# The last head pair's rows, stored in transfers of 64 rows and loaded with sixteen rows outermost

## The chip, the cores and the metric

The kernel runs on one core of a Trainium2 chip. The metric is the device time of one execution in microseconds (us). The kernel before was run three times: 1737.94 us at the median, from 1737.83 to 1739.5. A separate execution was recorded by the hardware profiler; all numbers of the trace are from it.

The engines in the tables are PE (TensorE, matrix multiplications; PEld is its loading of weights), DVE (VectorE), ACT (ScalarE), POOL (GpSimd) and SP (SyncE, which here only issues transfers). The data of every transfer is moved by sixteen DMA engines that the core has, whichever engine issues it.

## The reference

The output mixes two branches of the same input `x` (2048 x 512) by a gate per row:

```
g = sigmoid((x * gate_w).sum(-1))
q, k, v = heads(x @ wqkv)                    # 32 heads of 16
a = softmax(q k^T / 4) v, heads joined, @ wo # (2048 x 512)
b = Re(DFT over rows and columns of x)       # by matrices, (2048 x 512)
out = g * a + (1 - g) * b
```

The change touches only the last step of the branch `a`: the way in which the attention's result `o` of the last heads reaches the multiplication with `wo`.

## The kernel before

**Precision.** A float32 operand is split into a high part and a low part (names with `h` and `l`), and a product is made of three: high by high, high by low, low by high. So each operand of the output projection comes as a pair of blocks, each of 128 partitions by 512 columns.

**Attention.** The 32 heads are worked on in 16 pairs `p`, each in two halves `h` of 1024 queries, each half in 16 blocks of keys. One step is one such block: PE makes the scores (line 210), ACT their exponentials (lines 234 and 242), and PE, one or two steps later, adds up the values and the sums of the softmax in the bank `pvb` (line 755). At the end of a half, `quotients` copies `pvb` out and brings the sums into a small tile, and some steps later `divide` forms reciprocals, spreads them, and multiplies (POOL, line 777). POOL then splits the result into `oh` (line 784) and `ol` (line 787), 128 partitions each: two blocks `c` of 512 queries by two heads `j` of the pair by 32 partitions, of which the first 16 are the head's rows. Both are stored to `o_d` in DRAM (line 782), which is laid out as half, block of queries, pair in its group of four, 64 rows, 512 columns. Pairs up to 14 are stored from POOL's queue. Pair 15 (`NP - 1`) is stored from SP's; only its first half is, as its second half is used directly out of SBUF at the end.

**Output projection.** It contracts over the 512 rows of all heads. Heads of pairs 0 to 11 are read back as 128-row blocks (`output_rows`), multiplied by the weights `w2`. The last 8 heads are read back in blocks of two times 64 rows, one 64-row half for each of two blocks of queries: pairs 12 and 13 by `output_rest(h)`, pairs 14 and 15 by `output_last(h)`. Their weights `w4` are loaded in `output_operands`, with the same 64 rows twice. For `h = 1`, pair 15 is not in DRAM, so `output_last(1)` reads pair 14 alone, and the other rows are filled with zeros.

`halves_of` (line 185) multiplies the two 64-row halves separately. One group of output rows (`mix_some(t, (0, 1))`) has twelve such multiplications: six with the operands of `output_rest`, then six with those of `output_last`. In these six, the high part of both halves comes first, four times, and the low part of both last. The result is added to the output rows by DVE (`take_in`, line 867), and rows that are complete are stored from SP (line 940).

**Order.** Each engine carries out its instructions in the order in which the program writes them. The main loop does, for each step, the scores, the values, and one piece of the list `outputs()`, so that the pieces of the projection stand between the attention's steps on PE. The groups of row blocks 8, 9 and 10 (half 1) come first, then those of 0, 1 and 2 (half 0), all within the last pair's second half. Group 8 needs what `output_last(1)` loads, called in the step in which `divide` has stored pair 14's second half; group 0 needs what `output_last(0)` loads, called right behind the `divide` of pair 15's first half. SP issues all its transfers in one line, and each of its DMAs carries one of eight semaphores in turn. A load that reads rows which a store wrote waits for that store.

Of the kernel before, what the change touches and what calls it, by code (L numbers as in the profile page):

```python
# [10 lines left out]
F32 = mybir.dt.float32  # L11
# [11 lines left out]
DH = 16  # L23
NP = H // 2
NB = S // P
ND = D // P
# [27 lines left out]
def build(tc, xT, wqkv, wo, wrT, wiT, cr, ci, gate, out):  # L54
    nc = tc.nc
    with ExitStack() as ctx:
# [15 lines left out]
        o_d = [[dram.tile([2, 2, NP // ND, 64, 512], F32, name=f"o_d{f}_{i}") for i in range(2)] for f in range(ND)]  # L72
# [114 lines left out]
        def block(i):  # L187
            return big.tile([P, 512], F32R, tag=f"b{i}", name=f"b{i}")
# [62 lines left out]
        with ExitStack() as pf:  # L251
# [381 lines left out]
            with ExitStack() as py:  # L633
# [36 lines left out]
                for n, (ph, t, u) in enumerate(coef):  # L670
# [17 lines left out]
                    if (ph, t, u) == (0, NB - 3, 0):  # L688
                        for i in range(2):
                            raw = stk.tile([P, 4, D], F32, tag="stk", name="early")  # L690
# [13 lines left out]
                    for w in range(CS):  # L704
                        s = u * CS + w
# [24 lines left out]
        with ExitStack() as pa:  # L730
# [40 lines left out]
            def divide(p, h, ob, lc):  # L771

                nc.vector.reciprocal(lc, lc)  # L773
                nc.gpsimd.dma_start(r_d[p][h].rearrange("n (s e) -> (n s) e", e=16), lc)  # L774
                for n, (c, j, r) in enumerate(quads):
                    nc.gpsimd.dma_start(rb[r:r + DH, :], r_d[p][h][n:n + 1, :].to_broadcast([DH, 512]))
                nc.gpsimd.tensor_mul(ob, ob, rb)
                oh, ol = (ap.tile([P, 512], F32R, tag=tag, name=tag) for tag in ("oh", "ol"))
                queue = nc.sync if p == NP - 1 else nc.gpsimd

                def store(i, s):
                    queue.dma_start(o_d[p // 4][i][h, :, p % 4], s.bitcast(F32))

                nc.gpsimd.tensor_copy(oh, ob)
                if p == NP - 1:
                    store(0, oh)
                nc.gpsimd.tensor_sub(ol, ob, oh.bitcast(F32))
                if p < NP - 1:
                    store(0, oh)
                store(1, ol)  # L790
# [8 lines left out]
            def output_operands():  # L799

                for n in range(2 * ND - 2):
                    b = [block(6 + 2 * n + i) for i in range(2)]
                    raw = (ap.tile([P, D], F32, tag="craw", name="wor", bufs=2) if n == ND - 2 else
                           ap.tile([P, D], F32, tag="take", name="wor", bufs=3))
                    if n < ND - 1:
                        nc.sync.dma_start(raw, wo[n * P:n * P + P, :].rearrange("(h e) m -> e h m", e=DH))
                    else:
                        base = D - (8, 4, 2)[n - ND + 1] * DH
                        if n == ND:
                            for r in (0, 64):  # L810
                                nc.sync.dma_start(raw[r:r + 64, :], wo[base:base + 64, :])
                        elif n > ND:
                            nc.vector.memset(raw, 0.0)
                            for c, j, r in quads:
                                nc.sync.dma_start(raw[r:r + DH, :], wo[base + DH * j:base + DH * j + DH, :])
                        else:
                            for r in (0, 64):
                                nc.sync.dma_start(raw[r:r + 64, :],
                                                  wo[base:base + 64, :].rearrange("(h e) m -> e h m", e=DH))
                    raws_.append((raw, b))  # L820
                    if n % (ND - 1) == ND - 2:
                        yield
                        yield
                        for raw, b in raws_:
                            yield
                            nc.vector.tensor_copy(b[0], raw)
                            nc.vector.tensor_sub(b[1], raw, b[0].bitcast(F32))
                            (w2 if n < ND - 1 else w4).append(b)
                        raws_.clear()
                        yield  # L830
# [17 lines left out]

            def output_last(h):

                a, n = [block(28 + 2 * h + i) for i in range(2)], 2 - h
                for i in range(2):
                    for c in range(2):
                        src = o_d[ND - 1][i][h, c, 2:2 + n].rearrange("p (j r) s -> (p j) r s", j=2)
                        nc.sync.dma_start(a[i][64 * c:64 * c + 32 * n, :].bitcast(F32), src[:, 0:DH])
                        if n == 1:
                            nc.vector.memset(a[i][64 * c + 32:64 * c + 64, :].bitcast(F32), 0.0)
                direct[h].append(a)

            def load_y(c):  # L860
# [122 lines left out]

            now = [0]
            fill, operands = outputs(), output_operands()
            halves, halved, pend = [], [], []

# [17 lines left out]
            for step in range(NP * PERIODS):  # L1005
                p, i = step // PERIODS, step % PERIODS
                h, kb = i // NB, i % NB
# [40 lines left out]
                if halved and halved[0][0] <= step:  # L1048
                    p_, h_ = halved[0][1][:2]
                    divide(*halved.pop(0)[1])  # L1050
                    if p_ == NP - 2:
                        output_rest(h_)
                    if p_ == NP - 2 + (h_ == 0):
                        output_last(h_)
# [76 lines left out]
```

## Time and profile before

| What | Value |
|---|---|
| Median of three runs | 1737.94 us (1737.83 to 1739.5) |
| The profiled execution, its own time | 1739.11 us |
| Span of the trace in it | 1737.3 us |
| Mean granted clock of TensorE | 0.995 of full |
| Data moved | 195.53 MB, 113 GB/s on average |
| Stores from POOL of `oh` / `ol`, 30 each, issue to landing (median) | 13.5 / 14.3 us |

The span is the time from the first to the last recorded instruction; the profiled execution's time is a little longer. In the chain of waits, each piece is the work that the next piece waited for, back from the end; what lies in it sets the time. In the timelines, a row is a run of like instructions of one engine, with its start, its length, the line, the operation, the output and inputs with their shapes, and, in brackets, how long the engine had been idle before and what ended it. For a DMA the time in SP's row is that of its issue, not of its data.

### The profile page before, as it was taken

The page shows a single profiled execution, that of the slowest core. Times are in us where ns is not written, and L with a number is a line of the kernel's source. Part 1 is how long each engine was busy: PE and PEld are TensorE (multiplying, and loading weights), DVE is VectorE, ACT ScalarE, POOL GpSimd, SP SyncE. Part 2 cuts the span into 40 slices and gives each one's busy share as a digit, 9 for nine tenths or more (in the row PEclk, how much of TensorE's full clock was granted, in tenths as well). Part 3 has the DMA queues.
Part 4 walks back from the last instruction along what each step waited for, and adds up shares of the span by engine and source line. Part 5 has one row for each costly group of instructions (what it writes and reads, how often), then busy time and mean ns, then how long its engine had stood idle before and what let it go on. Part 6 is the DMA issues. An engine that isn't in the chain of part 4 may idle for free.

```text
span 1737.3 us, 36050 instructions
## 1 busy us (share of the span) xinstructions
PE 1715.8 (99%) x13656; PEld 1036.7 (60%) x13656; DVE 1090.2 (63%) x2062; ACT 1507.3 (87%) x2489; POOL 652.1 (38%) x774
## 2 busy tenths in 40 slices
PE   9999999999999999999999999999999999999996
PEld 6878888889888885333333333333455555555552
DVE  5898888999999996666666666666412112213332
ACT  6448889888888888999999999999988888888883
POOL 3672436655555751223242322324223222322231
PEclk9999999999999999999999999999999999999998
DMA  7783557544337663233342250441414335264713
GB/s 253 246 279 75 164 154 217 148 114 116 109 107 207 153 125 69 50 61 62 59 76 49 57 103 22 81 96 24 88 56 115 88 81 93 71 185 119 182 32 116
DMA packets 126522, 195.53 MB, mean 113 GB/s; under 512 B 55964, under 2 KB 58508, under 8 KB 119436
## 3 DMA queue, kind: packets, MB, share of 16 engines
q1 hardware_dynamic: 85164, 171.64, 37.5%
q0 software_dynamic: 40608, 20.54, 5.7%
q8 instruction: 107, 1.75, 0.4%
q10 hardware_dynamic: 576, 1.05, 0.2%
q14 instruction: 67, 0.55, 0.1%
HBM read 130.55 MB, written 63.18 MB: 112 GB/s over the span
## 4 chain that ended last, share of the span: by engine, by line
PE 94%; DMA 2%; DVE 1%; issue 1%; POOL 0%; ACT 0%; SPq 0%; DVEq 0%; POOLq 0%; ACTq 0%
PE pvb L755 28%; PE xy L185 25%; PE s L210 18%; PE s L154 9%; PE s L185 9%; PE s L135 5%; DVE fold L160 1%; DMA o_d<-ol 1%; DMA raws<-xT 0%; DMA q_d<-eh 0%; DMA raws<-wqkv 0%; DMA b<-o_d 0%; PE s L554 0%; DVE y L867 0%; ACT fold L158 0%
## 5 line engine op out<-in xcount | busy, mean ns | idle before, releaser
L234 ACT ACTIVATE eb<-s 128x1024 f32<-128x1024 f32 x512 | 576.4, 1126 | 77.6 <-PE s L210 77.5
L242 ACT ACTIVATE e<-s 128x512 f32<-128x512 f32 x1022 | 606.1, 703 | 0.4 <-PE s L210 0.4
L137 DVE TENSOR_REDUCE mx<-s 128x2 f32<-128x1024 f32 x364 | 441.4, 1224 | 187.5 <-PE s L135 187.2
L755 PE MATMUL pvb<-eb,va 128*17 128x512 f32 x2052 | 514.7, 599 | 0.0
L755 PE MATMUL pvb<-e,va 128*17 128x512 f32 x2044 | 513.8, 599 | 0.0
L160 DVE CUSTOM_DVE_ANT_0 fold<-s,fold 128x512 f32<-128x512 f32 x660 | 443.7, 690 | 52.7 <-PE s L154 24.8
L158 ACT ACTIVATE fold<-s 128x512 f32<-128x512 f32 x660 | 390.4, 604 | 72.8 <-PE s L154 50.3
L210 PEld LDWEIGHTS s<-qs,ks 50*128 50x128 f32 x2048 | 214.1, 185 | 356.1 <-ACT eb L234 254.9
L210 PE MATMUL s<-qs,ks 50*128 50x512 f32 x2048 | 421.0, 435 | 0.0
L185 PE MATMUL xy<-b,c 64*128 64x512 f32 x2448 | 396.1, 392 | 0.1
L154 PE MATMUL s<-ks,qs 48*128 48x512 f32 x1320 | 314.5, 405 | 1.6 <-DVE mx L160 1.0
L185 PEld LDWEIGHTS xy<-b,c 64*128 64x128 f32 x2448 | 280.4, 187 | 18.2 <-issue 1.0
L154 PEld LDWEIGHTS s<-ks,qs 48*128 48x128 f32 x1320 | 172.3, 184 | 47.0 <-DVE mx L160 12.4
L774 POOL DMA_DIRECT2D r_d<-lc x31 | 18.1, 583 | 454.8 <-DVE lc L773 454.8
L755 PEld LDWEIGHTS pvb<-eb,va 128*17 128x17 f32 x2052 | 70.6, 96 | 192.3 <-issue 185.0
L135 PE MATMUL s<-ks,qs 48*128 48x512 f32 x728 | 146.7, 395 | 0.7 <-DVE mx L137 0.7
L767 POOL DMA_DIRECT2D lc<-ob x124 | 62.8, 514 | 160.2 <-DVE ob L764 160.0
L185 PE MATMUL xy<-w,b 64*128 64x512 f32 x768 | 115.3, 392 | 0.0
L365 POOL TENSOR_TENSOR c<-craw,c 128x512 fp32r<-128x512 f32 x84 | 109.5, 1303 | 6.7
L185 PE MATMUL s<-b,chi 64*128 64x512 f32 x654 | 102.9, 391 | 0.0
L364 POOL CAST c<-craw 128x512 fp32r<-128x512 f32 x84 | 53.3, 635 | 125.2 <-PE xy L185 121.9
L867 DVE SCALAR_TENSOR_TENSOR y<-s,g,y 128x512 f32<-128x512 f32 x49 | 35.9, 749 | 85.5 <-PE s L185 84.9
(133 smaller groups left out, 1512.4 us busy)
## 6 DMA issues: line engine op xcount, KB each, us to landing
qs<-q_d SPq DMA_DIRECT2D x66, 256.0 KB
craw<-ci SPq DMA_DIRECT2D x64, 256.0 KB
craw<-cr SPq DMA_DIRECT2D x60, 256.0 KB
ks<-k_d SPq DMA_DIRECT2D x44, 256.0 KB
qs<-q_d SPq DMA_DIRECT2D x66, 128.0 KB
ab_d<-ab SPq DMA_DIRECT2D x32, 256.0 KB
y_d<-y SPq DMA_DIRECT2D x32, 256.0 KB
o_d<-oh POOLq DMA_DIRECT2D x30, 256.0 KB, 13.5
```

Source lines behind the costliest of these rows:

```text
L135: nc.tensor.matmul(ps[:, j, :], qs[b:b + 48, qb * P:(qb + 1) * P], ks[b:b + 48, c * 512:(c + 1) * 512], start=True, stop=True)
L137: nc.vector.tensor_reduce(mx[p][:, :, qb, c], ps, axis=AX.X, op=ALU.max)
L154: nc.tensor.matmul(ps, qs[b:b + 48, qb * P:(qb + 1) * P], ks[b:b + 48, c * 512:(c + 1) * 512], start=True, stop=True)
L158: nc.scalar.activation(fold[j], ps, AF.Relu)
L160: nc.vector.tensor_tensor_reduce(out=fold[j], in0=ps, in1=fold[j], scale=1.0, scalar=-3.0e38, op0=ALU.add, op1=ALU.max, accum_out=mx[p][:, ...
L185: nc.tensor.matmul(ps[j], lhs[r], rhs[r], start=first, stop=last)
L210: nc.tensor.matmul(pss[j], ks[b:b + 50, kb * P:(kb + 1) * P], qs[b:b + 50, q0:q0 + 512], start=True, stop=True)
L234: nc.scalar.activation(e, ps, AF.Exp, scale=SCALE)
L242: nc.scalar.activation(e[j], pss[j], AF.Exp, scale=SCALE)
L365: sub(lo, raw, hi.bitcast(F32))
L755: nc.tensor.matmul(pvb[r:r + VC, :], va[:, kb, 2 * p + j, :], es[c][j], start=kb == 0, stop=kb == NB - 1, tile_position=(0, r))
L767: nc.gpsimd.dma_start(lc[32 * n:32 * n + 32, :], ob[r + DH:r + VC, :].rearrange("p (s e) -> p s e", e=16))
```

## The change

The store of the last pair is cut into two transfers of 64 rows. The loads of `output_last` read with the 16 rows of a head outermost, and the heads inside, so that row `r` of head `n` lies at partition 4r + n of its 64 instead of 16n + r; for the second half these are two loads of 16 rows, into every fourth partition, per block of queries, and the whole block is filled with zeros first. The weights of that group are loaded in the same order of rows as those of the group before it.

```diff
@@ divide
-                    queue.dma_start(o_d[p // 4][i][h, :, p % 4], s.bitcast(F32))
+                    if p < NP - 1:
+                        queue.dma_start(o_d[p // 4][i][h, :, p % 4], s.bitcast(F32))
+                        return
+                    for c in range(2):
+                        queue.dma_start(o_d[p // 4][i][h, c, p % 4], s[64 * c:64 * c + 64, :].bitcast(F32))
@@ output_operands
-                        if n == ND:
-                            for r in (0, 64):
-                                nc.sync.dma_start(raw[r:r + 64, :], wo[base:base + 64, :])
-                        elif n > ND:
+                        if n > ND:
...
@@ output_last
-                a, n = [block(28 + 2 * h + i) for i in range(2)], 2 - h
+                a = [block(28 + 2 * h + i) for i in range(2)]
                 for i in range(2):
+                    if h:
+                        nc.vector.memset(a[i].bitcast(F32), 0.0)
                     for c in range(2):
-                        src = o_d[ND - 1][i][h, c, 2:2 + n].rearrange("p (j r) s -> (p j) r s", j=2)
-                        nc.sync.dma_start(a[i][64 * c:64 * c + 32 * n, :].bitcast(F32), src[:, 0:DH])
-                        if n == 1:
-                            nc.vector.memset(a[i][64 * c + 32:64 * c + 64, :].bitcast(F32), 0.0)
+                        src = o_d[ND - 1][i][h, c, 2:4].rearrange("p (j r) s -> r (p j) s", j=2)
+                        if not h:
+                            nc.sync.dma_start(a[i][64 * c:64 * c + 64, :].bitcast(F32), src[0:DH])
+                        else:
+                            for j in range(2):
+                                nc.sync.dma_start(a[i][64 * c + j:64 * c + 64:4, :].bitcast(F32), src[0:DH, j])
                 direct[h].append(a)
```

Without its branch, the second group's weights (`n == ND`) take the one that the first group's take, whose source is `wo[base:base + 64, :].rearrange("(h e) m -> e h m", e=DH)`.

## The prediction

> **What bounds the kernel now.** I read the page first, then the chain of waits in order of time, the timelines of PE and SP at the end, and last the busy time by stretches.
>
> ```profile
> PE 1715.8 (99%) x13656; PEld 1036.7 (60%) x13656; DVE 1090.2 (63%) x2062; ACT 1507.3 (87%) x2489; POOL 652.1 (38%) x774
> PE 94%; DMA 2%; DVE 1%; issue 1%; POOL 0%; ACT 0%; SPq 0%; DVEq 0%; POOLq 0%; ACTq 0%
> ```
>
> PE sets the time nearly everywhere, so an edit of transfers can only matter where PE waits for one. The 2% of DMA in the chain is where to look. In order of time, its late piece is this:
>
> ```profile
> 1685.96 0.61 POOL oh L784
> 1686.66 1.27 POOL ol L787
> 1687.95 11.67 DMA o_d<-ol
> 1700.22 4.87 DMA b<-o_d
> 1705.14 0.79 PE s L185
> 1706.79 3.54 PE pvb L755 x16
> 1710.99 1.39 PE s L185 x9
> 1712.38 0.50 PE s L210 x3
> 1712.87 1.84 PE pvb L755 x16
> 1715.37 1.38 PE s L185 x12
> ```
>
> (Start, length, what.) The chain leaves PE, runs through POOL's split of the pair into oh and ol, the store of ol (11.67 us), the load that reads it back (4.87 us), and only then returns to PE. The timeline of PE shows the hole that this makes:
>
> ```profile
> 1688.19 1.57 PE L185 MATMUL s<-b,b 64*128 64x512 f32 x12
> 1692.57 0.87 PE L185 MATMUL s<-b,b 64*128 64x512 f32 x6
> 1700.95 0.79 PE L185 MATMUL s<-b,b 64*128 64x512 f32 x1 [7.51 <-DMA b<-o_d]
> 1702.26 1.22 PE L185 MATMUL s<-b,b 64*128 64x512 f32 x3 [0.52 <-DMA b<-o_d]
> 1703.68 0.79 PE L185 MATMUL s<-b,b 64*128 64x512 f32 x1 [0.20 <-DMA b<-o_d]
> 1705.14 0.79 PE L185 MATMUL s<-b,b 64*128 64x512 f32 x1 [0.68 <-DMA b<-o_d]
> ```
>
> The twelve multiplications of an output group come in one burst (1688.19). For the group of row block 0 only six come (operands of pairs 12 and 13); the other six need what `output_last(0)` loads, and arrive one by one as its four loads land, 1.3 to 1.5 us apart. The hole runs from 1692.57 + 0.87 = 1693.44 to 1705.14: 11.7 us. The stretches show what else stands still, and what follows:
>
> ```profile
> 1680.00:1693.40 13.40, 13.40 (x112) 6.85 (x108) 4.23 (x6) 11.96 (x19) 5.10 (x7) 1.00 0.11 28
> 1694.50:1699.60 5.10, 0.00 (x0) 0.00 (x0) 0.00 (x0) 0.04 (x1) 0.00 (x0) 0.70 0.21 77
> 1699.60:1705.10 5.50, 2.79 (x5) 1.06 (x5) 0.00 (x0) 0.00 (x0) 0.00 (x0) 0.50 0.19 68
> 1705.10:1711.00 5.90, 5.86 (x27) 1.97 (x29) 1.41 (x2) 2.20 (x4) 0.00 (x0) 0.56 0.24 89
> 1711.00:1722.00 11.00, 11.00 (x92) 5.29 (x92) 2.82 (x4) 9.60 (x15) 0.00 (x0) 1.00 0.26 97
> ```
>
> (Length, busy PE, PEld, DVE, ACT, POOL, granted clock, share of the 16 DMA engines, GB/s.) During the hole every engine idles. The clock falls to 0.50 and is still 0.56 on average in 1705.1 to 1711, which is why sixteen value multiplications take 3.54 us there and 1.84 us later. So the hole costs more than its length.
>
> **What it costs.** A burst at full speed is followed by the next 1715.37 - 1710.99 = 4.38 us later; the one of block 0 starts at 1692.57 and the next at 1710.99, 18.42 us. The excess is 14.04 us: 11.7 of standing still, 2.3 of slow clock. This is the most that the change can give back at this place. ACT would not take over as the bound: in 1680 to 1693.4, at the same pace, it is busy 11.96 of 13.40 us with PE at 13.40.
>
> **The change part by part.** The stores of the last pair and the loads behind them, on SP:
>
> ```profile
> 1666.41 2.68 SPq L855 DMA_DIRECT2D b<-o_d  x4
> 1686.60 0.51 SPq L782 DMA_DIRECT2D o_d<-oh  x1
> 1687.95 0.51 SPq L782 DMA_DIRECT2D o_d<-ol  x1
> 1694.55 6.17 SPq L855 DMA_DIRECT2D b<-o_d  x4
> 1706.75 1.00 SPq L940 DMA_DIRECT2D out_dram<-y  x2
> ```
>
> SP issues the first load at 1694.55, when oh has landed (7.95 us after its issue), and ol lands at 1687.95 + 11.67 = 1699.6, only 5.1 us behind oh. So the two stores queue for the same engines, 256 KB take 5.1 us of them, and 7.95 - 5.1 = 2.85 us is the part that does not depend on bytes. Why 5.1 us: shares and rates of the DMA engines in stretches of the store and of two output stores, which have 128 rows outermost:
>
> ```profile
> 1686.60:1694.50 7.90, 6.84 (x58) 3.27 (x50) 1.62 (x3) 6.94 (x12) 1.27 (x1) 1.00 0.12 38
> 1707.50:1709.10 1.60, 1.60 (x12) 0.34 (x8) 0.00 (x0) 0.90 (x2) 0.00 (x0) 0.50 0.88 328
> ```
>
> A share of 0.12 is two engines of sixteen, and the store's outermost count is 2; the output stores use 0.88 and move 256 KB in about 0.8 us each. The loads land 1.3 to 1.5 us apart at a share near 0.2, with an outermost count of 4. The new stores have 64 outermost and the new loads 16, so I spread both over sixteen engines: 128 KB take 5.1 / 2 x 2/16 = 0.32 us as a store and 1.4 x 4/16 = 0.35 us as a load.
>
> [...]
>
> The part that does not depend on bytes isn't shown for this form. From above it is 2.85 us; from below 1.71 us, that of POOL's small store, with 1.94 us for its read back:
>
> ```profile
> 1679.00 1.71 DMA r_d<-lc
> 1682.45 1.94 DMA rb<-r_d
> ```
>
> I take 2.2 us, between, nearer the small ones, since the output stores' bytes are all there 1709.1 - 1706.75 = 2.4 us after the first issue though these are two of twice the size. Then, with 0.51 us for an issue: oh is ready at 1686.57, its halves are issued at 1686.60 and 1687.11; ol's at 1687.95 and 1688.46. The last half lands at 1688.46 + 2.2 + 0.32 = 1690.98. Each load waits for its own half alone in the built program, so the last one is issued at about 1691.03 and lands at 1691.03 + 2.2 + 0.35 = 1693.6. PE wants it as the last of the six: 1693.44 + 5 x 0.116 = 1694.0 (twelve take 1.39 us). The wait is gone, with 0.4 us to spare. With 2.85 us the last load lands at 1691.63 + 0.05 + 3.2 = 1694.9, a wait of 0.9 us; with 1.71, at 1692.6, none. A wait that short does not lower the clock here:
>
> ```profile
> 1724.10:1725.00 0.90, 0.04 (x2) 0.02 (x1) 0.75 (x3) 0.17 (x1) 0.66 (x1) 1.00 0.00 0
> 1725.70:1730.00 4.30, 4.30 (x37) 3.28 (x36) 2.69 (x5) 2.50 (x5) 1.77 (x2) 1.00 0.34 125
> ```
>
> PE stands for 0.86 of these 0.90 us and goes on at 1.00. [...]
>
> **The rest of the edit.** `output_last(1)`, which reads pair 14 back, gets eight loads of 16 rows instead of four of 32, and two fills of 128 rows instead of four of 32:
>
> ```profile
> L857 DVE MEMSET b<- x4: 485/485/485, 1648.1 to 1650.0; 32x512 f32 x4
> L813 DVE MEMSET wor<- x1: 485/485/485, 1596.5 to 1596.5; 128x512 f32 x1
> 1679.45 1.57 PE L185 MATMUL s<-b,b 64*128 64x512 f32 x12
> ```
>
> A fill of 128 rows takes 485 ns as one of 32 does, so DVE saves 2 x 0.485 = 0.97 us, off the path. The loads start behind POOL's store of pair 14 as now (1666.41). Eight issues at 2.68 / 4 = 0.67 us end at 1671.8, and with 2.85 us the last lands by 1675. PE wants them in the second half of the burst at 1679.45, from 1680.1. The cover is 5 us. What SP holds next is the store of oh, ready only at 1686.57. Each DMA waits for the eighth before it on its semaphore (the built order has eight in turn), and all of these are long done. The weights of the second group keep their count of issues and of rows, in another order; nothing near them is late. POOL's stores of the other pairs keep their form. The order on PE, ACT and POOL is unchanged. What was behind the hole, out to the last stores, moves forward as a whole.
>
> **Sum.** The profiled execution took 1739.11 us, 1.8 around its span of 1737.3. Its span becomes 1737.3 - 14.0 = 1723.3, its time 1725.1. It lies 1.2 us over the median of the runs, 1737.94, so the median becomes 1737.94 - 14.04 = 1723.9 us.
>
> **Rivals.**
> - A part of the wait stays (chance 0.11). If store and load each took 4.87 us after their issue, as the last load does now though it queues behind others, the last half would land at 1688.97 + 4.87 = 1693.8 and its load, issued by 1694.4, at 1699.3: 5.3 us of wait, and up to 2.3 us of slow clock. Then 1723.9 + 5.3 to 7.6 = 1729 to 1731.5. For it: no row shows this form alone. Against it: DMA is nearly idle there (0.12).
> - The form doesn't spread (0.04): the engines stay two and four, the same bytes queue on them, and the hole stays: 1737.9. Against it stands the share of 0.88 of stores with many rows outermost.
> - Slower (0.04): the eight 16-row loads into every fourth partition, a form that no row shows, run one behind the other. At 4.87 us each they end at 1666.4 + 39 = 1705.4; PE stands from 1680.1 for 25 us, with 2.3 of slow clock, while the later hole is covered by this one: 1737.9 - 14.0 + 27.6 = 1751.5. It decides from the point where the new hole costs more than 14 us, (1680.1 + 11.7 - 1666.4) / 8 = 3.2 us for each. Against it: the four loads of twice the size in the same place are used by PE without a wait today.
>
> **How the numbers follow.** The forecast, no wait or up to 0.9 us of it, has 0.81: 1723 to 1725.5 with the spread of the runs shown (1.7 us). The range reaches up to the first rival's lower end: 1722.0 to 1729.0. About 0.2% (3.5 us) is what a measurement tells from no change; faster has 0.81 + 0.11 = 0.92, same 0.04, slower 0.04.
>
> **What would show it.** Right: the burst of block 0 has all twelve multiplications together, no idle of PE before the chain's last transposes, granted clock 1.00 from 1680 to the end, a DMA share well over 0.2 in the 3 us after the store of oh, loads issued before 1692. Wrong: six multiplications alone with idle time ended by b<-o_d, at this group or at the one of block 8 (at 1680), or a hole of some other cause once this one is gone, such as PE waiting for ACT.

## The result, and the profile after

| | Before | After |
|---|---|---|
| Median of six runs each (us) | 1738.84 (1737.83 to 1739.5) | 1726.32 (1725.69 to 1727.06) |
| Profiled execution: time / span (us) | 1739.11 / 1737.3 | 1727.06 / 1725.1 |
| Mean granted clock | 0.995 | 0.999 |

The ratio of the times is 0.9929, with a 95% interval of 0.9916 to 0.9942: the change makes the kernel 12.5 us faster. The forecast was 1723.9 us, 2.4 us too low, and the range of 1722 to 1729 us holds the result.

From the page of the kernel after, busy time by engine, and the chain of waits by engine:

```profile
PE 1711.2 (99%) x13656; PEld 1039.2 (60%) x13656; DVE 1089.1 (63%) x2060; ACT 1507.0 (87%) x2489; POOL 653.0 (38%) x774
PE 95%; DMA 1%; DVE 1%; issue 1%; ACT 1%; POOL 0%; SPq 0%; DVEq 0%; POOLq 0%; ACTq 0%
```

DMA's share of the chain went from 2% to 1%. PE is busy 4.6 us less with the same instructions, as fewer of them run at a slow clock (mean granted 0.999 against 0.995). The timeline of PE at the place of the hole (start, length, line, operation, shapes, count, idle time before it):

```profile
1680.09 1.57 PE L185 MATMUL s<-b,b 64*128 64x512 f32 x12
1688.82 1.54 PE L185 MATMUL s<-b,b 64*128 64x512 f32 x12
1693.20 1.10 PE L185 MATMUL s<-b,b 64*128 64x512 f32 x7
1694.52 1.07 PE L185 MATMUL s<-b,b 64*128 64x512 f32 x5 [0.22 <-DMA b<-o_d]
1698.39 1.55 PE L185 MATMUL s<-b,b 64*128 64x512 f32 x12
```

The burst of row block 0 (1693.20) is almost whole. Its twelve multiplications end at 1694.52 + 1.07 = 1695.59, so they take 2.39 us, where an undisturbed burst takes 1.57: 0.82 us of small waits for the loads are left. The row shows 0.22 of it in one piece; beside it the view of waits has 0.7 us at the loading of weights (PEld). From here on, "excess" is the time from the start of this burst to the start of the next, less the 4.38 us of an undisturbed one. It is 1698.39 - 1693.20 - 4.38 = 0.81 us. (The prediction took the second start from the chain and got 14.04 for the kernel before. The timeline of PE alone, used for all kernels below, has that burst at 1710.83 and gives 1710.83 - 1692.57 - 4.38 = 13.88; this is its row in the kernel before:)

```profile
1710.83 1.54 PE L185 MATMUL s<-b,b 64*128 64x512 f32 x12
```

The timeline of SP, which issues the transfers:

```profile
1666.62 4.92 SPq L862 DMA_DIRECT2D b<-o_d  x8
1687.34 1.11 SPq L786 DMA_DIRECT2D o_d<-oh  x2
1688.70 1.09 SPq L786 DMA_DIRECT2D o_d<-ol  x2
1689.91 2.48 SPq L859 DMA_DIRECT2D b<-o_d  x4
```

Before, the first load was issued 7.95 us behind the store of oh; now it is 2.57 us (1689.91 - 1687.34), and the four loads are issued in one piece. The stretches before, at and behind the place (length; busy PE, PEld, DVE, ACT, POOL; granted clock; share of the DMA engines; GB/s):

```profile
1680.00:1693.40 13.40, 13.40 (x114) 7.20 (x112) 4.23 (x6) 11.93 (x19) 5.36 (x8) 1.00 0.31 82
1693.40:1697.00 3.60, 3.38 (x28) 1.67 (x28) 1.37 (x2) 2.91 (x5) 0.00 (x0) 1.00 0.08 28
1697.00:1710.00 13.00, 13.00 (x110) 5.92 (x98) 2.85 (x5) 10.66 (x17) 0.00 (x0) 1.00 0.33 122
```

PE is busy throughout but for 0.22 us, and the clock stays at 1.00, where it had fallen to 0.50.

**Where the 12.2 us of span came from.** The excess went from 13.88 to 0.81: 13.07 us. Against that, the profiled execution of the kernel after reaches this place later than that of before: the bursts at 1679.45 and 1688.19 before start at 1680.09 and 1688.82 after, 0.64 and 0.63 us late. Comparing PE's instructions one by one, this shift arises in the first 100 us and stays constant from there to the hole. It is of that execution and not of the change: in a second profile of the same kernel (the repeat, below) the burst starts at 1688.02, 0.17 us early. 13.07 - 0.63 = 12.4, against 12.2 of span; where the other 0.2 went was not followed.

### The profile page after: what moved, and what is told of

Same layout as the page of the kernel before. It is cut to its first block, busy times and chain, and to the rows that moved or that the text cites. A ratio compares the mean times of both kernels' runs of the same rounds, so it can differ in the third digit from the quotient of the medians.

```text
span 1725.1 us, 36058 instructions
## 1 busy us (share of the span) xinstructions
PE 1711.2 (99%) x13656; PEld 1039.2 (60%) x13656; DVE 1089.1 (63%) x2060; ACT 1507.0 (87%) x2489; POOL 653.0 (38%) x774
## 3 DMA queue, kind: packets, MB, share of 16 engines
q8 instruction: 107, 1.75, 0.4%
## 4 chain that ended last, share of the span: by engine, by line
PE 95%; DMA 1%; DVE 1%; issue 1%; ACT 1%; POOL 0%; SPq 0%; DVEq 0%; POOLq 0%; ACTq 0%
PE pvb L755 28%; PE xy L185 25%; PE s L210 18%; PE s L154 10%; PE s L185 9%; PE s L135 5%; DMA q_d<-eh 0%; DMA raws<-wqkv 0%; DVE fold L160 0%; DMA b<-o_d 0%; PE s L554 0%; DVE y L872 0%; ACT fold L158 0%; DVE s L278 0%; DVE mx L137 0%
## 5 line engine op out<-in xcount | busy, mean ns | idle before, releaser
L154 PE MATMUL s<-ks,qs 48*128 48x512 f32 x1320 | 314.4, 405 | 1.7 <-DVE mx L160 1.0
L154 PEld LDWEIGHTS s<-ks,qs 48*128 48x128 f32 x1320 | 172.7, 184 | 46.9 <-DVE mx L160 12.7
L135 PE MATMUL s<-ks,qs 48*128 48x512 f32 x728 | 151.7, 394 | 1.1 <-DVE mx L137 0.7
L890 DVE CAST chi<-craw 128x512 fp32r<-128x512 f32 x40 | 19.7, 493 | 111.7 <-PE s L185 83.2
```

The lines of the kernel that those rows point to most:

```text
L135: nc.tensor.matmul(ps[:, j, :], qs[b:b + 48, qb * P:(qb + 1) * P], ks[b:b + 48, c * 512:(c + 1) * 512], start=True, stop=True)
L154: nc.tensor.matmul(ps, qs[b:b + 48, qb * P:(qb + 1) * P], ks[b:b + 48, c * 512:(c + 1) * 512], start=True, stop=True)
```

## The experiments

### Only the store

The kernel before, with the store cut in two and nothing else:

```diff
-                    queue.dma_start(o_d[p // 4][i][h, :, p % 4], s.bitcast(F32))
+                    if p < NP - 1:
+                        queue.dma_start(o_d[p // 4][i][h, :, p % 4], s.bitcast(F32))
+                        return
+                    for c in range(2):
+                        queue.dma_start(o_d[p // 4][i][h, c, p % 4], s[64 * c:64 * c + 64, :].bitcast(F32))
```

> Only the store of the last pair is cut in halves of 64 rows; loads and weights are those of before. Excess here means: from the start of the burst of group 0 to that of group 1, less 4.38 us (before 14.04, after the change 1698.56 - 1693.20 - 4.38 = 0.98). Theory (both forms take their time from the number of engines they spread over): the stores land as after the change, by 1691.5; the four loads on four engines queue at 1.35 us each and land at about 1693.3, 1694.7, 1696.0 and 1697.4, against 1694.1 wanted: a hole of about 3.4 us, excess 3.4 to 5.5 us, time 1728.5 to 1731. Rival (the store alone makes the gain, the form of the loads is hidden): excess 1, time 1726. Rival (the store's form is nothing without the loads'): excess 12 or more, time over 1737.

1732.2 us (1730.8 to 1733.16), ratio 0.9961 [0.9946, 0.9975]. The timeline of PE, and one row of the chain of waits:

```profile
1692.37 1.12 PE L185 MATMUL s<-b,b 64*128 64x512 f32 x7
1694.58 0.74 PE L185 MATMUL s<-b,b 64*128 64x512 f32 x3 [1.08 <-DMA b<-o_d]
1695.90 0.50 PE L185 MATMUL s<-b,b 64*128 64x512 f32 x1 [0.58 <-DMA b<-o_d]
1697.18 0.49 PE L185 MATMUL s<-b,b 64*128 64x512 f32 x1 [0.78 <-DMA b<-o_d]
1702.13 1.55 PE L185 MATMUL s<-b,b 64*128 64x512 f32 x12
```

```profile
1698.14 3.49 PE pvb L755 x16
```

The long wait for the store is gone. The four loads, in the form in which each raised its semaphore four times in the kernel before (a share of the DMA engines of 0.21 here in 1692 to 1697.5), let PE go on 1.3 us apart (1694.58, 1695.90, 1697.18), as the prediction read them in the kernel before. The excess is 1702.13 - 1692.37 - 4.38 = 5.38 us: the store alone gives back 13.88 - 5.38 = 8.5 us. Behind waits of 1.08, 0.58 and 0.78 us with three and one multiplications between them the clock is slow: 0.62 is granted in 1697.5 to 1702, and the sixteen value multiplications behind them take 3.49 us, nearly as long as behind the long hole (3.54).

### Only the loads

The kernel after, with the old store, `queue.dma_start(o_d[p // 4][i][h, :, p % 4], s.bitcast(F32))`, for every pair.

> Only the loads and the order of the weights' rows are new; the store is one transfer of 2 x 64 rows, as before. Theory: the store still holds two engines for 2 x 5.1 us, ol lands near 1700.4, and the loads behind it land by 1703.6: a hole of about 9.7 us with the slow clock behind it, excess about 12 us, time 1736 to 1738, no gain that can be told. Rival (the loads alone make the gain): excess under 3, time under 1729.

1737.02 us (1736.31 to 1737.87), ratio 0.9987 [0.9977, 0.9996]. The timeline of PE, then the chain:

```profile
1692.62 0.87 PE L185 MATMUL s<-b,b 64*128 64x512 f32 x6
1700.02 1.54 PE L185 MATMUL s<-b,b 64*128 64x512 f32 x4 [6.53 <-DMA b<-o_d]
1702.33 1.61 PE L185 MATMUL s<-b,b 64*128 64x512 f32 x2 [0.77 <-DMA b<-o_d]
1708.23 1.54 PE L185 MATMUL s<-b,b 64*128 64x512 f32 x12
```

```profile
1688.00 11.68 DMA o_d<-ol
1699.75 2.53 DMA b<-o_d
```

The store of ol takes 11.68 us as before (11.67), and the load behind it 2.53 us instead of 4.87. The excess is 11.23 us, so the loads alone give 2.65. The two parts alone make 8.5 + 2.65 = 11.1 us, together they make 13.07. Part of the difference is the clock: with only one of them it still falls behind the wait (0.62 granted in 1697.5 to 1702 with the store alone, a mean of 0.996 over the run here, against 0.999 with both; sixteen value multiplications take 3.49 us with the store alone and 2.94 here, instead of 1.84). The rest was not taken apart.

### One store over all partitions

Here the last pair has an area of its own in DRAM, whose rows are one dimension of 128, so that the store is one transfer of 128 rows. The rows of pair 14 in its loads are fetched earlier, with those of the other half; late are only the 32 rows of pair 15 in each block of queries. The weights follow this order of rows.

```diff
+        o15_d = [dram.tile([P, 512], F32, name=f"o15_d{i}") for i in range(2)]
...
-                    for c in range(2):
-                        queue.dma_start(o_d[p // 4][i][h, c, p % 4], s[64 * c:64 * c + 64, :].bitcast(F32))
+                    queue.dma_start(o15_d[i], s.bitcast(F32))
...
+                            src = o15_d[i][64 * c:64 * c + 64, :].rearrange("(j r) s -> r j s", j=2)
+                            nc.sync.dma_start(a[i][64 * c + 32:64 * c + 64, :].bitcast(F32), src[0:DH])
```

> The store of the last pair is one transfer of 128 rows into its own 128-row area, so two issues fewer on SP, and pair 14's rows of the first half are loaded early, so that the four late loads have 32 rows each. The wait of about 1 us that is left after the change has two theories. If it is the line of eight issues on SP (0.55 us each), the last load is issued and lands about 1 us earlier: excess 0 to 0.3 us. If it is the one DMA engine that carries PE's next 16 KB of instructions (0.93 us, begun 1692.11 in the trace after), the last load still waits for that engine: excess 0.3 to 1.0 us. Time 1725.3 to 1726.5 in either, so the trace tells it, not the time.

1725.15 us (1725.06 to 1726.18), ratio 0.9923 [0.9906, 0.9939]. The timelines of SP and PE (the helper has moved to line 186):

```profile
1686.29 0.33 SPq L786 DMA_DIRECT2D o_d<-oh  x1
1687.65 0.33 SPq L786 DMA_DIRECT2D o_d<-ol  x1
1688.36 2.47 SPq L869 DMA_DIRECT2D b<-o_d  x4
```

```profile
1692.26 1.54 PE L186 MATMUL s<-b,b 64*128 64x512 f32 x12
1696.62 1.55 PE L186 MATMUL s<-b,b 64*128 64x512 f32 x12
```

The excess is 1696.62 - 1692.26 - 4.38 = -0.02 us: nothing is left of the wait. One store is issued in 0.33 us, two halves in 1.1. The median is 1.2 us below that of the kernel after; their intervals overlap, but the trace shows where the 0.8 us comes from.

### Two stores, with pair 14 still fetched early

The last kernel, with its store in two halves of 64 rows.

> As e3, pair 14's rows loaded early and the four late loads of 32 rows each, but with the store in two transfers of 64 rows as in the change. It tells what of e3's gain is the single store. If the two halves cost their issues, excess is 0.4 to 1.0 us, as after the change; if the smaller loads made e3's gain, 0 to 0.2.

1725.58 us (1725.24 to 1725.83), ratio 0.9923 [0.9908, 0.9938]. The timeline of PE:

```profile
1692.27 1.95 PE L186 MATMUL s<-b,b 64*128 64x512 f32 x12
1697.03 1.57 PE L186 MATMUL s<-b,b 64*128 64x512 f32 x12
```

The excess is 0.38 us. So by these profiles two halves instead of one transfer cost 0.4 us, and the loads of half the rows account for the other 0.4 of the 0.81. Each is one profile, and two profiles of the kernel after differ by 0.3 (below); but SP's rows agree: here the first load is issued 2.54 us behind the store of oh, with one transfer 2.07.

### Four stores

The kernel after, each store in four transfers of 32 rows:

```diff
-                        queue.dma_start(o_d[p // 4][i][h, c, p % 4], s[64 * c:64 * c + 64, :].bitcast(F32))
+                        for j in range(2):
+                            queue.dma_start(o_d[p // 4][i][h, c, p % 4, 32 * j:32 * j + 32],
+                                            s[64 * c + 32 * j:64 * c + 32 * j + 32, :].bitcast(F32))
```

> The changed kernel with each store of the last pair in four transfers of 32 rows: the same bytes, the same sixteen engines, four issues more. If SP's line of issues (0.55 us each) sets when the loads go out, the last load goes out some 1.4 to 2.2 us later and excess rises from 0.98 to 2.4 to 3.2 us, time 1.4 to 2.2 us over the changed kernel's. If it does not, and the engine that carries PE's instructions is the whole of the wait, excess stays near 1.0.

1729.04 us (1727.69 to 1729.42), ratio 0.9944 [0.9927, 0.996]. The timelines of SP and PE:

```profile
1686.49 1.73 SPq L787 DMA_DIRECT2D o_d<-oh  x4
1688.31 1.80 SPq L787 DMA_DIRECT2D o_d<-ol  x4
1690.22 3.26 SPq L861 DMA_DIRECT2D b<-o_d  x4
```

```profile
1692.42 1.23 PE L185 MATMUL s<-b,b 64*128 64x512 f32 x7
1694.12 1.26 PE L185 MATMUL s<-b,b 64*128 64x512 f32 x4 [0.46 <-DMA b<-o_d]
1695.71 0.50 PE L185 MATMUL s<-b,b 64*128 64x512 f32 x1 [0.33 <-DMA b<-o_d]
1699.01 1.57 PE L185 MATMUL s<-b,b 64*128 64x512 f32 x12
```

The excess is 2.21 us, 1.4 more than with two halves, and between the two expectations. SP's rows show two delays. An issue of 32 rows takes 0.44 us, and the line of eight puts the first load 3.73 us behind the store of oh instead of 2.57: 1.16 us. Then the four loads take 3.26 us to issue instead of 2.48. The second of them takes 1.24 us instead of 0.55, and the fourth waits for the last part of ol, which lands 3.23 us after its issue, while fifteen of the sixteen increments of its semaphore are there after 1.72. A transfer of 16 KB of the kind "instruction", begun at 1690.54, runs then (1.9% of 16 engines in 1690 to 1694, which is 1.2 us on one engine); the run with 48 multiplications, below, shows a store that met one. So the line of issues is real, and it cost 1.16 us here. The other 0.8 us came with one late engine; the kernel after has a share of that too (0.5 to 0.9 us, below), so that the difference of the two is 1.4.

### The projection's step put off

The kernel after, in which the piece of the projection that holds this burst is taken half a step later, so that the loads have more time:

```diff
-                if step >= MIX and step % 2 == 0:
+                if step >= MIX and step % 2 == 0 and step != DEFER:
...
+                    if step == DEFER and _ == 0:
+                        next(fill)
```

> The changed kernel with the second half of group 0 put 1.4 us later in PE's order, behind the scores and half of the values of its step; nothing else is moved. If the 1 us left after the change is PE waiting for the loads, whatever makes them late, PE is 13.9 to 14.2 us ahead of the kernel before behind this place (after the change: 13.07, with the offset of the start taken out), time 0.5 to 1.1 us under the changed kernel's. If the 1 us is something else, such as the burst itself being slower, it stays at 13.1.

1726.73 us (1725.86 to 1727.69), ratio 0.993 [0.9915, 0.9945]: no gain on the kernel after. The timeline of PE, with the scores (line 211) beside the projection:

```profile
1693.27 0.87 PE L186 MATMUL s<-b,b 64*128 64x512 f32 x6
1694.32 0.98 PE L211 MATMUL s<-qs,ks 50*128 50x512 f32 x4 [0.18 <-ACT eb L235]
1696.22 0.96 PE L186 MATMUL s<-b,b 64*128 64x512 f32 x6
```

PE no longer waits for the loads, but the next scores wait for ACT's exponentials, which come later now (0.18 us in the row). PE is then 12.7 to 12.9 us ahead of the kernel before, not the 13.9 to 14.2 expected. So of the 13.88 us this order leaves out 1.1, about as much as the kernel after (0.81 us, and 1.12 in its repeat); how much of the 1.1 beyond the 0.18 is due to ACT was not taken apart.

### The program's code shifted

What remained open was why the last loads come late in the kernel after, when the DMA engines had so little to do. The view of the DMA engines for 1692 to 1696, in 40 bins of 0.1 us, and its row for the queue of instructions:

```profile
GB/s 143 205 451 144 143 205 164 246 287 266 144 143 184 287 307 266 185 82 0 21 20 41 21 20 20 21 0 0 0 0 0 0 0 0 0 0 0 0 0 0
q8 instruction: 1, 0.02, 1.4%
```

The loads move at 140 to 310 GB/s up to 1693.7 (the 451 holds the 16 KB named next), and from 1693.8 on for another 0.8 us at 20 GB/s. The share of the DMA engines in 1693.8 to 1694.6 is 0.06, which is one engine of sixteen (the old store had 0.12 and moved 38 GB/s): fifteen are done, one is not. In the same stretch the view shows one transfer of 16 KB of the kind "instruction", 1.4% of 16 engines for 4 us, which is 0.9 us on one engine. The trace's single packets put its start at 1692.22, in the middle of the loads. Each of the four loads raises its semaphore sixteen times as its parts land; in the first the sixteenth increment comes 0.07 us behind the fifteenth, in each of the last three 0.7 to 1.1 us. There are 107 transfers of instructions of this size in the run, one in 16 us. The trace does not show for which engine they are. The author's estimate is that they are PE's and come as PE advances: 1.75 MB over PE's 27,312 instructions (13,656 multiplications and as many loads of weights) is 64 bytes each.

If so, instructions added ahead on PE move the moment at which the engine is held. Small multiplications were added to the warm-up at the start of the kernel after (48, 25 and 16 of them), into a bank that only the warm-up uses there:

```diff
+                for n in range(25):
+                    nc.tensor.matmul(warm[0:VC, n % 2, 0:P], ident[:, 0:VC], ident, start=True, stop=True)
```

With 48:

> The changed kernel with 48 small multiplications (17 columns of weights) ahead of the warm-up, which move PE's later instructions by 48 x 2 x 64 bytes, 6 KB of the 16 KB that one instruction transfer carries. If the wait left is the engine held by that transfer, the transfer comes about 5.8 us earlier (near 1686 before the shift of the start), ahead of the stores, and excess falls to 0 to 0.2 us. If it is the line of issues on SP, excess stays at 0.9 to 1.0 us. The start may cost up to 5 us more, so the time is not judged.

1735.99 us, ratio 0.9983 [0.9974, 0.9992]. The added multiplications make the start of the program longer; at this place PE is 7.9 us later for it. They are 96 multiplications and 96 loads of weights at PE, by the same estimate 12 KB of instructions and not the 6 KB reckoned with. The timeline of PE, and one row of the chain of waits:

```profile
1701.12 1.41 PE L185 MATMUL s<-b,b 64*128 64x512 f32 x7
1707.34 1.57 PE L185 MATMUL s<-b,b 64*128 64x512 f32 x12
```

```profile
1701.29 2.69 DMA b<-o_d
```

The excess is 1.84 us, neither of the values expected. The transfer of instructions now began at 1688.74, some 11 us earlier against PE, and met another step of the same chain, the small store of the sums' reciprocals from POOL. First this row of POOL's timeline in the kernel after, then that in this kernel:

```profile
1681.64 1.94 POOL L776 DMA_DIRECT2D rb<-r_d  x4 [1.41 <-DMA r_d<-lc]
```

```profile
1691.05 1.94 POOL L778 DMA_DIRECT2D rb<-r_d  x4 [2.92 <-DMA r_d<-lc]
```

The wait for that store is 2.92 us instead of 1.41: fifteen increments of its semaphore are there 1.71 us after its issue, the sixteenth after 3.21. Everything behind it is 1.5 us late; take that off the 1.84, and 0.3 is left. This alone proves little of the loads, so two more shifts followed, and the unchanged kernel once more.

With 25 and with 16 (one execution each; 1728.66 and 1727.94 us, with the longer start):

> As e4 with 25 small multiplications instead of 48. With none the transfer of PE's instructions begins 4.8 to 5.2 us after the store of oh is issued, with 48 it began 8.0 us before it, so 0.27 us each: with 25 it should begin about 1.8 us before the store and be over when it is issued, where no other transfer runs. If the held engine is part of the wait that is left, excess falls from 1.0 (1.12 in the repeat) to 0.2 to 0.5 us; if the line of issues is the whole, it stays at 0.9 to 1.2.

> As e4 with 16 small multiplications: the transfer of PE's instructions should begin about 0.7 us after the store of oh is issued and hold one engine while the stores run. If the held engine costs what waits for it, one of the stores lands up to 1 us late, the loads behind it too, and excess is 0.9 to 1.5 us; if the line of issues is the whole, 0.9 to 1.2 as well, so this run alone tells nothing of the two; it shows whether the store is hit.

The kernel after, repeated:

> The changed kernel once more, beside the others. Excess 0.7 to 1.1 us, time 12 to 13 us under the kernel before. If the transfer of PE's instructions falls at another moment in this execution, excess goes with it: without it in the 3 us of the loads 0.2 to 0.5 us.

The DMA view of the kernel with 25, 1693 to 1697 (its loads come 2 us later), in bins of 0.1 us:

```profile
GB/s 184 266 82 41 41 102 102 143 266 328 246 185 164 143 225 205 246 144 143 184 184 307 348 164 185 184 205 184 184 225 144 41 20 0 0 0 0 0 0 0
```

The tail at the rate of one engine is gone, and the view lists no transfer of instructions in this stretch; by the packets it began at 1686.80, before the stores. The timelines of PE with 25, with 16, and of the repeat:

```profile
1695.50 1.78 PE L185 MATMUL s<-b,b 64*128 64x512 f32 x12
1700.10 1.54 PE L185 MATMUL s<-b,b 64*128 64x512 f32 x12
```

```profile
1694.45 1.88 PE L185 MATMUL s<-b,b 64*128 64x512 f32 x12
1699.15 1.54 PE L185 MATMUL s<-b,b 64*128 64x512 f32 x12
```

```profile
1692.39 1.09 PE L185 MATMUL s<-b,b 64*128 64x512 f32 x7
1693.94 1.14 PE L185 MATMUL s<-b,b 64*128 64x512 f32 x5 [0.46 <-DMA b<-o_d]
1697.89 1.54 PE L185 MATMUL s<-b,b 64*128 64x512 f32 x12
```

The excess is 0.22 us with 25 and 0.32 with 16; in the two profiles of the kernel after it is 0.81 and 1.12. The run with 16 was a miss: it was to hold the engine during the stores, for 0.9 to 1.5 us, but the transfer began at 1688.23, 0.3 us before the first store was issued, and no store took more than 0.2 us longer from issue to landing than in the kernel after. Both shifts agree that the wait is short when the transfer of instructions does not fall into the loads. The burst starts 3.3 to 3.4 us behind the issue of the first load in all four executions of the table, so the shifts gave the loads no more time. The repeat took 1726.72 us (1726.01 to 1726.9), ratio 0.9929 [0.9914, 0.9944], as the first time.

| Kernel | Transfer of instructions begins | First store issued | Four loads issued | Excess (us) |
|---|---|---|---|---|
| After | 1692.22 | 1687.34 | 1689.91 to 1692.39 | 0.81 |
| After, repeated | 1691.73 | 1686.49 | 1689.05 to 1691.53 | 1.12 |
| 25 added | 1686.80 | 1689.57 | 1692.11 to 1694.59 | 0.22 |
| 16 added | 1688.23 | 1688.51 | 1691.18 to 1693.66 | 0.32 |

## Why the prediction was right, and where it was off

**The hole and its price.** Right. The store on two engines was the long wait (alone it gives 8.5 us), the loads on four engines most of what is left then (5.38 us of excess against 0.81), and the slow clock went with them. The clock is 1.00 over the whole of the place, as forecast, and the short waits that are left did not lower it. Two of the prediction's signs came only in part: the twelve multiplications come as seven and five, and the clock is not 1.00 "to the end", but 0.90 in 1710 to 1725, as at the end of the kernel before (0.90 in 1722 to 1737.3).

**The forms spread.** Right. From 1692 to 1693.7 the DMA engines move 140 to 310 GB/s for the loads, where the old store moved 38, and the share in 1680 to 1693.4 went from 0.11 to 0.31. The semaphores agree: the old store of oh gets two increments when its data land (7.88 and 7.90 us after its issue), each old load four, and each new store and load sixteen.

**Halves or one transfer.** Against one transfer whose outermost count is 2 the halves are far better: the store alone gives back 8.5 us. Against one transfer of 128 rows they are worse, by the 0.4 us between the two experiments with pair 14 fetched early. Most of this is the second issue: in the run with two halves the second half of oh is issued 0.53 us behind the first and lands 0.64 us behind it, so little is left for halves that hold each other up.

**No wait left.** This step failed, by 0.8 to 1.1 us, and three of its terms were off. The largest is the landing of the last load: "1691.03 + 2.2 + 0.35 = 1693.6", 2.55 us from the issue. In the chain of waits of the kernel after, this is the load that PE waits for first:

```profile
1690.56 3.92 DMA b<-o_d
```

This load, the second, took 3.92 us. By the increments of its semaphore the last one took 3.21 us, 2.48 without its slowest engine. So 2.55 was about right for fifteen engines; what was missing is that the load landed with its slowest engine, 0.73 us behind the fifteen others, with a transfer of instructions of 0.93 us begun at 1692.22. Measured by the shifts this is worth 0.5 to 0.9 us (0.81 or 1.12 against 0.22 or 0.32).

The second term is the issue. The last load was issued at 1691.84, 0.2 us later than forecast once the 0.63 of the later start are added.

The third is the time at which PE wants it: "1693.44 + 5 x 0.116 = 1694.0", 1.45 us after the burst's start at 1692.57. The runs put it at 1.02 to 1.04. With 48 added multiplications the last load lands at 1701.29 + 2.69 = 1703.98, 2.86 us after the burst's start at 1701.12, and the excess is 1.84. In the kernel after it lands at 1691.84 + 3.21 = 1695.05, 1.85 us after the start, with an excess of 0.81. The prediction counted on from the end of the sixth multiplication, but these overlap: at 0.116 us each the twelfth starts 11 x 0.116 = 1.28 us after the first. The rest is by the author's estimate the loading of its weights, at which the view of waits has 0.7 us for the same data (PEld); that was not measured apart. So the "0.4 us to spare" was not there. With the engine free the last load lands 2.7 us after its issue, and the 0.2 to 0.3 us of excess that stay with 25 and 16 are mostly this term.

That fewer and smaller transfers remove all of the wait is shown, even with a transfer of instructions in the loads (begun at 1690.62 in the run with one store); which of the two does more is not. The upper bound of the prediction, 2.85 us and 0.9 us of wait, covered the result, though for other reasons than those that hold: in that it was lucky.

**The sum.** The excess of 14.04 us was read from two views and should have been 13.88. Of the 2.4 us between forecast and result, 0.9 are the baseline, which was 1737.94 us over three runs and is 1738.84 over six, and 1.0 is what was not given back (14.04 - 13.07). The other 0.5 (1738.84 - 13.07 = 1725.8, against 1726.32) are within the spread of the runs.

**What was costed at nothing.** Right. The eight loads of `output_last(1)` are issued in 4.92 us instead of 2.68, and the burst that uses them (1680.09) has its twelve multiplications in 1.57 us, without a wait. The fills and the order of the weights show no shift. ACT did not become the bound here; PE does wait for it when its own order is changed, if only for 0.18 us in the row of the step put off.

**The rivals.** A wait that stays at 5.3 us or more did not come with the whole change: in the kernel after, stores and loads land 2.2 to 3.9 us after their issue, not 4.87. The other two fell: the forms spread, and the eight loads of 16 rows are in time.

## What to carry to other kernels

Where the chain of waits goes through a transfer, look at its outermost count before its bytes: 256 KB with an outermost count of two went over two engines (two increments, a share of 0.12), and PE stood still for 11.7 us while fourteen DMA engines had little to do. Repair the store and the load behind it together, since a wait that is only shortened can cost the slow clock all the same (0.62 granted behind the waits of the store alone). When the wait is down to about a microsecond, count the issues in the queue, count the time at which PE wants the data from the start of its burst and not from the end of its rows (1.02 to 1.04 us here), and leave 1 us for the slowest of the sixteen engines (0.7 to 1.1 us behind the others here); fetch early whatever is already there, and store what is late in one transfer with many rows outermost.

## What the runs showed of the hardware

- The page of the kernel after lists 107 transfers of the kind "instruction" on one queue, of 16 KB each: by their packets 0.9 to 1.9 us long (1.1 at the median), one in some 16 us. Some transfers in flight while one ran got the sixteenth increment of their semaphore late on its own: 0.7 to 1.1 us behind the fifteenth for three of the loads in the kernel after, and 1.5 us for a small store in the run with 48 added multiplications and for the last part of ol in the run with four stores. Multiplications added at the start of the program moved the wait near its end: with 48 the small store was waited for 2.92 us instead of 1.41, with 25 and 16 the excess was 0.22 and 0.32 us instead of 0.81 and 1.12. That the instructions are PE's is an estimate, from their 64 bytes for each of PE's and from their coming some 11 us earlier against PE with 192 instructions added on PE; the packets of the trace don't name the engine that carries them.
- As their data landed, the transfers issued by SP raised their semaphores two times with an outermost count of two (the old store, with a share of the DMA engines of 0.12), four times with four (the old loads, 0.19), and sixteen times with 16, 64 and 128 (the new loads and stores, 0.82 in 1689.3 to 1691.6, and the output stores, 0.88 in the kernel before). In the three loads of the kernel after whose sixteenth increment came late, one engine of sixteen was busy meanwhile (a share of 0.06 in 1693.8 to 1694.6).
- Behind three waits of 1.08, 0.58 and 0.78 us, with three and one multiplications between, the granted clock was 0.62 in the run with the store alone, and 3.49 us went on what takes 1.84; behind the wait of 11.7 us in the kernel before it was 0.56 and 3.54 us, and behind a single one of 0.86 us there it was 1.00.
